# One linear-attention and two-layer kernel: q times kv in three float32r passes, k's maximum row by a transpose, lower parts of blocks 0 and 1 made by TensorE

## The chip, the cores and the metric

The kernel runs on one core of a Trainium2 chip. The metric is the device time of one execution in microseconds. The time before is a median of three runs.

## The reference, cut to what matters

```python
# q, k, v: (8, 8, 576, 64)
q_s = exp(q - max(q, -1)); q_s = q_s / (sum(q_s, -1) + 1e-9)      # over the 64 features
k_s = exp(k - max(k,  2)); k_s = k_s / (sum(k_s,  2) + 1e-9)      # over the 576 rows
kv  = einsum('bhsd,bhse->bhde', k_s, v)
x   = einsum('bhsd,bhde->bhse', q_s, kv)                          # then (4608, 512)
h = x @ w_in;  x1 = where(h > 0, h, exp(min(h, 0)) - 1) @ w_out   # 512 -> 2048 -> 512
h = x1 @ w2_in; out = (P(h) / Q(h)) @ w2_out                      # 512 -> 2048 -> 512
```

All tensors are float32; the weights and the second layer's coefficients are inputs as well.

## The kernel before

The 4608 rows of x are nine blocks of 512 columns (x is kept transposed, features on the partitions). A batch has 576 rows, so block j covers the end of batch j-1 and the beginning of batch j: `pieces(j)` gives the two parts, 16j and 128-16j groups of four columns, that is 64 and 448 columns in block 1, 128 and 384 in block 2, and so on to 448 and 64 in block 7; blocks 0 and 8 are one piece. A block has four pairs of heads (`hp`), of 128 features each.

`plan_pair` makes one pair of one block. For k: the maximum over the rows on VectorE (`k_max`), a transpose on TensorE (`k_maxT`), a maximum over its columns (`k_top`), the result spread into a row for all partitions by a float32 product with the identity (`k_row`, L418), the subtraction (`k_sub`) and the exponential (`k_exp`); `kv_mm` (L433) multiplies with v and a column of ones, `kv_norm` makes the reciprocal, and `kv_div` writes the two 64x64 blocks of the block-diagonal `kvd` on ScalarE (L447) or VectorE (L449). For q: `q_max` to `q_mul` make the softmax, `q_T` (L479) transposes it by four TensorE transposes into a PSUM bank, `q_copy` (L483) copies it out, and `x_mm` (L490) multiplies it with `kvd` in float32. The trace shows a float32 product as two rows and a transpose or a float32r product as one.

Everything after that is float32r: a number is kept as an upper part, which is the float32r rounding (`copy_hi`, L202, on ScalarE), and a lower part, the rest (`sub_lo`, L205, on VectorE or GpSimd), and a product is three passes, upper by upper, upper by lower, lower by upper. `plan_in` (L564 to L566) makes h of 128 hidden features (a step f) in a bank, 12 passes of 512 columns; `plan_elu` makes relu, exp, elu (L673) and the two parts of g; `plan_out` (L605) adds 12 passes into four accumulators. 16 steps make a block. Blocks 0 and 1 take turns, eight steps each, while the weights are loaded and split: `plan_w1` turns two steps' weights at a time into the two parts by VectorE operations on their bits (L232, L241, L246, L251, L255 and L205). The other blocks follow one after the other, and then the second layer, nine blocks again.

The order on every engine is made at build time by `Plan`: each operation has engines with costs, operations it follows, a rank, and buffers that it takes and frees, and the planner issues whichever can start first by its own clock. On the chip each engine then runs its own queue in that order, and waits for others by semaphores. `bank` stands for four PSUM banks, `xs` for eight buffers of an x tile with its two parts, `qe` for the only buffer of the exponential of q.

Of the kernel before, what the change touches and what calls it, by code (L numbers as in the profile page):

```python
# [18 lines left out]
P = 128  # L19
# [84 lines left out]
def linear_attention_elu_rational(  # L104
# [58 lines left out]
    kvd = [at.tile([P, P], F32, name=f"kvd{i}") for i in range(6)]  # L163
# [3 lines left out]
    for name, cap in (("m", 2), ("e", 4), ("bank", 4), ("acc", 4), ("xs", 8), ("gs", 2), ("x", 1), ("st", 1), ("kt", 1),  # L167
                      ("vb", 1), ("qt", 1), ("ke", 1), ("qe", 1), ("km", 2), ("top", 2), ("qT", 1), ("kvd", 6), ("hc", 3),
                      ("s", 3), ("p", 3), ("g2", 2), *((f"w{f}_{i}", 1) for f in range(KF // 2) for i in range(2))):
        plan.kind(name, cap)  # L170
# [178 lines left out]

    def plan_pair(j, hp, r, gate=None):  # L350
# [54 lines left out]
        def k_max(e):  # L405
            km = b["km"] = at.tile([P, 2, D], F32, tag="km", name="km", bufs=2)
            nc.vector.tensor_reduce(out=km, in_=b["kt"].rearrange("p h j d -> p h d j"), op=ALU.max, axis=AX.X)
# [9 lines left out]
        def k_row(e):  # L417
            nc.tensor.matmul(b["mt"][:, P:2 * P], b["top"].to_broadcast([P, P]), ident, start=True, stop=True)  # L418
# [24 lines left out]
        def kv_div(e):  # L443
            for o in (0, 64):
                dst, src, rs = kvd[n % 6][o:o + 64, o:o + 64], b["pk"][o:o + 64, 0:D], b["rs"][o:o + 64]
                if e == "ACT":
                    nc.scalar.activation(out=dst, in_=src, func=AF.Copy, scale=rs)  # L447
                else:
                    nc.vector.tensor_scalar(out=dst, in0=src, scalar1=rs, scalar2=None, op0=ALU.mult)  # L449
# [26 lines left out]
        def q_T(e):  # L476
            pt = b["pt"] = bank()
            for i in range(4):
                nc.tensor.transpose(pt[:, i * P:(i + 1) * P], b["qe"][:, i].rearrange("p h d -> p (h d)"), ident)  # L479

        def q_copy(e):
            b["qT"] = f32_tile("qT", 1, at)
            nc.scalar.activation(out=b["qT"], in_=b["pt"], func=AF.Copy)  # L483

        def x_mm(e):
            px = b["px"] = bank()
            pv = px.rearrange("c (i p) -> c i p", i=4)
            t = b["qT"].rearrange("c (i p) -> c i p", i=4)
            for bb, p0, p1 in pieces(j):
                nc.tensor.matmul(pv[:, :, p0:p1], kvd[(bb * NP + hp) % 6], t[:, :, p0:p1], start=True, stop=True)  # L490

        def x_hi(e):
            x = x_tile[0, j, hp] = main.tile([P, 2, TB], F32R, tag="xs", name="xs", bufs=8)
            copy_hi(x[:, 0], b["px"])
# [14 lines left out]
        t1 = chain("q_T", (PE(0.47), q_T, [o], r + 1.5), take=["bank", "qT"], free=[("qe", qx)], extra=0.2)  # L509
        qc = chain("q_copy", (ACT(), q_copy, [t1], r + 1.7), free=[("bank", t1)], extra=ahead)  # L510

        if j < B:
            pad = chain("pad_k", (DVE(0.2) if first else POOL(0.3), pad_k, (), r - 4 if first else r - 3), take=[kkind])
            l = chain("load_k", ((("SP", 1.1),), load_k, [pad], r - 3), extra=DMA)
            lv = chain("load_v", ((("ACT" if first else "SP", 1.9),), load_v, (), r - 0.6 if first else r - 2), take=[vkind], extra=DMA)
            km = chain("k_max", (DVE(0.8), k_max, [l, gate], r - 0.5), take=["km"])
            mt = chain("k_maxT", (PE(0.2), k_maxT, [km], r - 0.45), take=["bank"], extra=0.2, free=[("km", km)])
            top = chain("k_top", (DVE(0.3), k_top, [mt], r - 0.4), take=["top"], extra=ahead)
            o = chain("k_row", (PE(0.3), k_row, [top], r - 0.35), extra=0.2, free=[("top", top)])
            o = chain("k_sub", (DVE(0.85), k_sub, [o], r + 0.1), free=[("bank", mt)])  # L520
            kx = o = chain("k_exp", (ACT(0.75), k_exp, [o], r + 0.2), take=["ke"], free=[(kkind, pad)], extra=ahead)
            kvm = chain("kv_mm", (PE(1.15), kv_mm, [o, lv], r + 0.5), take=["bank", "kvd"], extra=0.2,
                        free=[("ke", kx), (vkind, lv)])
            o = chain("kv_norm", (DVE(0.4), kv_norm, [kvm], r + 0.7))
            kv_ready[n] = chain("kv_div", ((("ACT", 0.6), ("DVE", 0.4)), kv_div, [o], r + 0.7), free=[("bank", kvm)],
                                extra=ahead)
            kvd_of[n] = kvm
        free = [("qT", t1)]
# [3 lines left out]
        xm = chain("x_mm", (PE(0.9), x_mm, [qc] + need, r + 2), take=["bank", "xs"], extra=0.2, free=free)  # L532
        o = chain("x_hi", (ACT(), x_hi, [xm], r + 2.1))
        x_ready[0, j, hp] = chain("x_lo", (DVE(), x_lo, [o], r + 2.2), free=[("bank", xm)])
        x_owner[0, j, hp] = "xs", xm
# [309 lines left out]
    with tc.manual_schedule():  # L845
# [3 lines left out]
        make_identity(nc, ident)  # L849
        for t in kvd:  # L850
            nc.vector.memset(t, 0.0)
# [57 lines left out]
```

## Time and profile before

| | us |
|---|---|
| median of 3 runs (1730.26 to 1730.96) | 1730.64 |
| the profiled execution | 1730.37 |
| its span in the trace | 1728.6 |
| TensorE busy | 1683.9 |
| VectorE busy | 1075.0 |
| ScalarE busy | 1013.1 |
| GpSimd busy | 822.9 |

The profiled execution lasts 1.8 us longer than its span. TensorE rows overlap (a row of 512 columns reads 390 ns long, and the next begins some 227 ns after it), so what a product costs is read from the starts of the rows around it and not from its length.

### The profile page before, as it was taken

What the parts mean: (1) busy time and instruction counts of PE and PEld (TensorE: products, weight loads), DVE (VectorE), ACT (ScalarE), POOL (GpSimd) and SP (SyncE); (2) the same over time, 40 slices, a digit from 0 to 9 for tenths busy, and PEclk for the clock granted to TensorE, in tenths of its full rate; (3) what the DMA queues carried; (4) which work ended last, traced back from release to release, by engine and by line L of the source; (5) the groups of instructions that cost most, each with busy time, mean ns of one, the idle gap of its engine ahead of it and who ended that gap; (6) DMA issues with size and microseconds to landing.
All of it is one profiled execution on the core that took longest, in us unless ns stands there. A gap on an engine that the chain in (4) does not pass through costs nothing.

```text
span 1728.6 us, 21977 instructions
## 1 busy us (share of the span) xinstructions
PE 1683.9 (97%) x7920; PEld 1372.6 (79%) x7920; DVE 1075.0 (62%) x1500; ACT 1013.1 (59%) x1696; POOL 822.9 (48%) x619
## 2 busy tenths in 40 slices
PE   4799999999999999999999999999999999999999
PEld 3577888888888888888888788888888888888887
DVE  7999656454454544432123867776768676868686
ACT  3565545454444544434456767776868686868675
POOL 2324433433333334323365756564747475757553
PEclk8899999999999999999999999999999999999999
DMA  9710343232322333210233001010101010101000
GB/s 281 253 53 26 124 138 101 76 106 71 110 81 68 103 87 113 69 43 7 74 103 109 26 2 48 1 43 1 49 1 49 1 50 0 50 1 38 0 25 25
DMA packets 110925, 112.58 MB, mean 65 GB/s; under 512 B 48864, under 2 KB 82656, under 8 KB 110816
## 3 DMA queue, kind: packets, MB, share of 16 engines
q1 hardware_dynamic: 106016, 110.00, 20.3%
q10 hardware_dynamic: 4800, 1.18, 0.3%
q8 instruction: 62, 1.02, 0.2%
q14 instruction: 47, 0.39, 0.1%
HBM read 81.79 MB, written 29.36 MB: 64 GB/s over the span
## 4 chain that ended last, share of the span: by engine, by line
PE 88%; DVE 6%; DMA 2%; issue 1%; ACT 1%; POOL 1%; SPq 0%; DVEq 0%; POOLq 0%; ACTq 0%
PE acc L605 43%; PE ps L564 14%; PE ps L566 14%; PE ps L565 14%; PE ps L490 2%; PE ps L433 1%; DMA bits<-in_moe_w_in_dram 1%; PE ps L479 1%; DVE bits L251 1%; DVE x L241 1%; DMA kt<-in_k_dram 0%; DVE x L232 0%; DVE x L255 0%; DVE bits L246 0%; POOL gs L205 0%
## 5 line engine op out<-in xcount | busy, mean ns | idle before, releaser
L564 PE MATMUL ps<-xs,w_in 128*128 128x512 f32 x1152 | 458.3, 398 | 2.8 <-DVE p L727 2.7
L605 PE MATMUL acc<-gs,w_out 128*128 128x512 f32 x1728 | 439.8, 400 | 12.6 <-ACT gs L202 7.7
L566 PE MATMUL ps<-xs,w_in 128*128 128x512 f32 x1152 | 450.8, 391 | 0.0
L565 PE MATMUL ps<-xs,w_in 128*128 128x512 f32 x1152 | 449.7, 390 | 0.0
L605 PEld LDWEIGHTS acc<-gs,w_out 128*128 128x128 f32 x1728 | 321.8, 190 | 85.4 <-ACT gs L202 9.2
L205 POOL TENSOR_TENSOR gs<-m,gs 128x512 fp32r<-128x512 f32 x127 | 173.3, 1364 | 353.8 <-ACT gs L202 304.1
L673 DVE SCALAR_TENSOR_TENSOR m<-m,ps 128x512 f32<-128x512 f32 x144 | 98.5, 684 | 273.5 <-ACT m L670 265.8
L564 PEld LDWEIGHTS ps<-xs,w_in 128*128 128x128 f32 x1152 | 217.3, 189 | 50.8 <-DVE p L727 4.1
L566 PEld LDWEIGHTS ps<-xs,w_in 128*128 128x128 f32 x1152 | 216.9, 188 | 46.5
L565 PEld LDWEIGHTS ps<-xs,w_in 128*128 128x128 f32 x1152 | 217.4, 189 | 44.9 <-issue 0.7
L709 POOL TENSOR_TENSOR s<-s,m 128x512 f32<-128x512 f32 x144 | 218.9, 1520 | 32.2 <-ACT m L698 32.2
L605 PE MATMUL acc<-w_out,g 128*128 128x512 f32 x864 | 211.6, 389 | 0.0
L605 PE MATMUL acc<-w_out,gs 128*128 128x512 f32 x864 | 210.6, 389 | 0.0
L667 ACT ACTIVATE m<-ps 128x512 f32<-128x512 f32 x144 | 85.8, 596 | 207.4 <-PE ps L566 173.4
L605 PEld LDWEIGHTS acc<-w_out,gs 128*128 128x128 f32 x864 | 162.5, 188 | 33.7
L605 PEld LDWEIGHTS acc<-w_out,g 128*128 128x128 f32 x864 | 162.2, 188 | 33.8 <-DVE g L205 0.3
L205 POOL TENSOR_TENSOR g<-p,g 128x512 fp32r<-128x512 f32 x71 | 105.2, 1481 | 173.5 <-ACT g L202 116.4
L718 DVE SCALAR_TENSOR_TENSOR s<-s,m 128x512 f32<-128x512 f32 x144 | 148.1, 1028 | 48.7 <-ACT m L715 34.5
L706 ACT ACTIVATE p<-ps,a_sb 128x512 f32<-128x512 f32 x144 | 112.2, 779 | 109.6 <-PE ps L566 50.6
L202 ACT ACTIVATE gs<-m 128x512 fp32r<-128x512 f32 x144 | 90.6, 629 | 143.5 <-PE acc L605 125.7
L724 DVE TENSOR_TENSOR p<-p,ps 128x512 f32<-128x512 f32 x144 | 98.2, 682 | 85.6 <-ACT s L702 76.5
L727 DVE SCALAR_TENSOR_TENSOR p<-p,a_sb,ps 128x512 f32<-128x512 f32 x144 | 107.3, 745 | 62.6 <-ACT m L698 62.3
(93 smaller groups left out, 2038.1 us busy)
## 6 DMA issues: line engine op xcount, KB each, us to landing
x<-e SPq DMA_DIRECT2D x36, 256.0 KB, 2.1
e<-x SPq DMA_DIRECT2D x36, 256.0 KB, 2.8
out_dram<-e SPq DMA_DIRECT2D x36, 256.0 KB, 2.6
kt<-in_k_dram SPq DMA_DIRECT2D x32, 256.0 KB, 2.8
bits<-in_moe_w_in_dram SPq DMA_DIRECT2D x16, 512.0 KB, 7.8
bits<-in_moe_w_out_dram SPq DMA_DIRECT2D x16, 512.0 KB, 9.7
st<-in_moe_w_in_dram SPq DMA_DIRECT2D x16, 512.0 KB, 4.2
w<-x SPq DMA_DIRECT2D x32, 256.0 KB, 2.1
```

The costliest lines, as they stand in the source:

```text
L202: nc.scalar.activation(out=hi, in_=src, func=AF.Copy)
L205: engine[e].tensor_tensor(out=lo, in0=src, in1=hi.bitcast(F32), op=ALU.subtract)
L564: nc.tensor.matmul(b["h"], w[:, 0, kk, :], x[:, 0], start=(kk == 0), stop=False)
L565: nc.tensor.matmul(b["h"], w[:, 0, kk, :], x[:, 1], start=False, stop=False)
L566: nc.tensor.matmul(b["h"], w[:, 1, kk, :], x[:, 0], start=False, stop=(kk == KD - 1))
L605: nc.tensor.matmul(o, lhsT, rhs, start=(f == f0 and n == 0), stop=(f == f1 and n == 2))
L673: nc.vector.scalar_tensor_tensor(out=b["m"], in0=b["m"], scalar=-1.0, in1=b["h"], op0=ALU.add, op1=ALU.max)
L706: nc.scalar.activation(out=b["p"], in_=b["h"], func=AF.Identity, scale=a_sb[:, 3:4], bias=a_sb[:, 2:3])
L709: engine[e].tensor_tensor(out=b["s"], in0=b["s"], in1=b["a"], op=ALU.add)
L718: nc.vector.scalar_tensor_tensor(out=b["s"], in0=b["s"], scalar=1.0 + 1e-6, in1=b["a"], op0=ALU.add, op1=ALU.mult)
L724: nc.vector.tensor_tensor(out=b["p"], in0=b["p"], in1=b["h"], op=ALU.mult)
L727: nc.vector.scalar_tensor_tensor(out=b["p"], in0=b["p"], scalar=a_sb[:, 1:2], in1=b["h"], op0=ALU.add, op1=ALU.mult)
```

## The change

`k_row` becomes a transpose of the same column. `x_mm` reads a q with two parts and a `kvd` with two parts and makes three float32r passes per piece; the float32 buffer `qT` is gone, and the two parts of q lie in the pair's `xs` buffer, which is now taken at `q_T` and not at `x_mm`. `kv_div` is an upper part on ScalarE (two instructions) and a lower part on VectorE (two instructions) for every pair. In blocks 2 to 8 the lower part of q is a subtraction on VectorE (`q_lo`). In blocks 0 and 1 (`PE_LO`) TensorE makes the lower parts of q and of x in a second bank: it makes the same sum again (four float32 products with the identity, or the three passes again), adds the upper part times minus the identity (`less`), and ScalarE copies what is left (`rest`). The costs given to the planner change with it.

```diff
+    minus = at.tile([P, P], F32R, name="minus")
+    kvd = [at.tile([P, 2, P], F32R, name=f"kvd{i}") for i in range(6)]
...
-            nc.tensor.matmul(b["mt"][:, P:2 * P], b["top"].to_broadcast([P, P]), ident, start=True, stop=True)
+            nc.tensor.transpose(b["mt"][:, P:2 * P], b["top"].to_broadcast([P, P]), ident)
...
+                nc.scalar.activation(out=hi, in_=src, func=AF.Copy, scale=rs)
+                nc.vector.scalar_tensor_tensor(out=lo, in0=src, scalar=rs, in1=hi.bitcast(F32),
+                                               op0=ALU.mult, op1=ALU.subtract)
...
+            if j in PE_LO:
+                pt = b["pt2"] = bank()
+                for i in range(4):
+                    nc.tensor.matmul(pt[:, i * P:(i + 1) * P], b["qe"][:, i].rearrange("p h d -> p (h d)"), ident,
+                                     start=i == 0, stop=False)
...
+        def less(ps):
+            def fn(e):
+                nc.tensor.matmul(b[ps], minus, x_tile[0, j, hp][:, 0], start=False, stop=True)
+            return fn
+
+        def rest(ps):
+            def fn(e):
+                nc.scalar.activation(out=x_tile[0, j, hp][:, 1], in_=b[ps], func=AF.Copy)
+            return fn
...
+            for ps in ("px", "px2") if j in PE_LO else ("px",):
+                b[ps] = bank()
+                pv = b[ps].rearrange("c (i p) -> c i p", i=4)
+                for bb, p0, p1 in pieces(j):
+                    kv = kvd[(bb * NP + hp) % 6]
+                    for m, (kk, qq) in enumerate(((0, 0), (0, 1), (1, 0))):
+                        nc.tensor.matmul(pv[:, :, p0:p1], kv[:, kk], t[:, qq, :, p0:p1],
+                                         start=m == 0 and (p0 == 0 or ps == "px"), stop=m == 2 and ps == "px")
...
+            o = chain("q_less", (PE(0.23), less("pt2"), [o], r + 1.8), free=[("bank", t1)], extra=0.2)
+            qc = chain("q_rest", (ACT(), rest("pt2"), [o], r + 1.9), free=[("bank", t1)])
+        else:
+            qc = chain("q_lo", (DVE(), q_lo, [o], r + 1.8), free=[("bank", t1)], extra=ahead)
...
-        xm = chain("x_mm", (PE(0.9), x_mm, [qc] + need, r + 2), take=["bank", "xs"], extra=0.2, free=free)
+        xm = chain("x_mm", (PE(1.4 if j in PE_LO else 0.7), x_mm, [qc] + need, r + 2), take=["bank"] * (2 if j in PE_LO else 1), extra=0.2, free=free)
```

TensorE's queue, from the products of block 0's second pair to the first step, before (L479 is the transposes of q, L490 x_mm, L433 kv_mm, whose last instance here is that of block 1's first pair, L411 and L418 the two of k, L564 the first step):

```order
L479 MATMUL ps<-ident,qe 128x128 x4
L411 MATMUL ps<-ident,km 128x128
L490 MATMUL ps<-qT,kvd_144 128x512
L479 MATMUL ps<-ident,qe 128x128 x4
L490 MATMUL ps<-qT,kvd_145 128x512
L418 MATMUL ps<-ident,top 128x128
L479 MATMUL ps<-ident,qe 128x128 x4
L433 MATMUL ps<-vb,ke 64x65 x10
L490 MATMUL ps<-qT,kvd_146 128x512
L564 MATMUL ps<-xs,w_in 128x512
```

The same queue of the changed kernel, from block 0's third pair to the first step (L484 is the transposes, L488 the float32 products of the second bank, L501 `less`, L517 x_mm, L437 kv_mm, again that of block 1's first pair, L602 the first step):

```order
L484 MATMUL ps<-ident,qe 128x128 x4
L488 MATMUL ps<-ident,qe 128x128 x4
L437 MATMUL ps<-vb,ke 64x65 x10
L501 MATMUL ps<-xs,minus 128x512
L517 MATMUL ps<-xs,kvd_146 128x512 x6
L501 MATMUL ps<-xs,minus 128x512
L484 MATMUL ps<-ident,qe 128x128 x4
L488 MATMUL ps<-ident,qe 128x128 x4
L602 MATMUL ps<-xs,w_in 128x512
```

Behind kv_mm of block 1's first pair stood one product, x_mm of the fourth pair; now `less`, six passes and `less` of the third pair and the transposes of the fourth stand there, and x_mm of the fourth pair has gone behind the beginning of the first step.

VectorE's queue at `kv_div` of the first pair, before (L439 and L440 are `kv_norm`, L468 and L469 `q_rec`, L415 `k_top` of the third pair):

```order
L439 TENSOR_SCALAR rs<-ps 128x1
L440 RECIPROCAL rs<-rs 128x1
L468 TENSOR_SCALAR sm<-sm 128x8
L469 RECIPROCAL sm<-sm 128x8
L415 TENSOR_REDUCE top<-ps 128x1
```

And in the changed kernel (L443, L444, L473, L474 and L419 are the same five; L453 is the lower part of `kvd`):

```order
L443 TENSOR_SCALAR rs<-ps 128x1
L444 RECIPROCAL rs<-rs 128x1
L473 TENSOR_SCALAR sm<-sm 128x8
L474 RECIPROCAL sm<-sm 128x8
L453 SCALAR_TENSOR_TENSOR kvd_144<-ps,rs,kvd_144 64x64 x2
L419 TENSOR_REDUCE top<-ps 128x1
```

Two instructions that read ScalarE's upper part now stand ahead of `k_top`; the same holds at all 32 pairs.

VectorE's queue around the thirteenth elu (L673, step 4 of block 1), before (L241, L246, L251 and L255 are the splitting of weights):

```order
L241 SCALAR_TENSOR_TENSOR x<-bits,x 128x1024
L232 TENSOR_SCALAR x<-bits 128x1024
L246 TENSOR_SCALAR bits<-bits 128x1024
L251 SCALAR_TENSOR_TENSOR bits<-bits 128x1024
L673 SCALAR_TENSOR_TENSOR m<-m,ps 128x512
L465 TENSOR_REDUCE sm<-qe 128x4x2
L255 TENSOR_TENSOR x<-x,bits 128x1024
L673 SCALAR_TENSOR_TENSOR m<-m,ps 128x512
```

And in the changed kernel (L711 is elu; L242, L247, L252 and L256 the same splitting):

```order
L242 SCALAR_TENSOR_TENSOR x<-bits,x 128x1024
L247 TENSOR_SCALAR bits<-bits 128x1024
L242 SCALAR_TENSOR_TENSOR x<-bits,x 128x1024
L252 SCALAR_TENSOR_TENSOR bits<-bits 128x1024
L247 TENSOR_SCALAR bits<-bits 128x1024
L256 TENSOR_TENSOR x<-x,bits 128x1024
L252 SCALAR_TENSOR_TENSOR bits<-bits 128x1024
L411 TENSOR_REDUCE km<-kt 128x128
L458 TENSOR_REDUCE mx<-qt 128x8
L711 SCALAR_TENSOR_TENSOR m<-m,ps 128x512
```

More of the splitting of weights stands ahead of this elu. Counted from the beginning of the queue to it, the changed kernel has 16 L453 more, the two `kv_div` of VectorE (L449) and eight lower parts of x (L205) less, one subtraction of q more (GpSimd had it), and one more each of the kinds L241, L246, L251 and L255.

## Rows read from the trace of the kernel before

**Rows 1.** The page's first line.

```profile
span 1728.6 us, 21977 instructions
```

**Rows 2.** Busy time by stretch: start:end us, length, each engine, granted TensorE clock.

```profile
16.00:153.00 137.00, 112.89 (x571) 85.02 (x568) 131.18 (x170) 76.36 (x118) 43.42 (x32) 0.91 0.50 162
72.00:82.00 10.00, 5.86 (x14) 4.18 (x14) 9.42 (x12) 4.51 (x7) 5.57 (x3) 0.50 0.81 272
153.00:850.00 697.00, 696.67 (x3511) 565.51 (x3511) 326.52 (x555) 318.43 (x553) 251.00 (x217) 1.00 0.27 82
```

**Rows 3.** Timeline of all engines at 149.0 to 152.8 us: start, length, engine, line.

```profile
149.12 0.68 DVE L673 SCALAR_TENSOR_TENSOR m<-m,ps 128x512 f32<-128x512 f32 x1
...
150.60 2.06 POOL L205 TENSOR_TENSOR gs<-m,gs 128x512 fp32r<-128x512 f32 x1 [3.21 <-ACT gs L202]
...
152.72 0.50 PE L605 MATMUL acc<-gs,w_out 128*128 128x512 f32 x1 [1.64 <-POOL gs L205]
```

**Rows 4.** TensorE's timeline around one k_maxT and one k_row of the long stretch.

```profile
307.49 0.27 PE L411 MATMUL ps<-ident,km 128*128 128x128 f32 x1
...
307.84 0.39 PE L565 MATMUL ps<-xs,w_in 128*128 128x512 f32 x1
308.07 0.40 PE L566 MATMUL ps<-xs,w_in 128*128 128x512 f32 x1
...
313.08 0.38 PE L418 MATMUL ps<-ident,top 128*128 128x128 f32 x2
...
313.53 0.39 PE L565 MATMUL ps<-xs,w_in 128*128 128x512 f32 x1
```

**Rows 5.** TensorE's timeline around x_mm of blocks 3 and 7.

```profile
325.70 1.02 PE L490 MATMUL ps<-qT,kvd 128*128 128x192 f32 x4
...
326.79 0.40 PE L565 MATMUL ps<-xs,w_in 128*128 128x512 f32 x1
...
718.98 1.08 PE L490 MATMUL ps<-qT,kvd 128*128 128x448 f32 x4
...
720.18 0.39 PE L565 MATMUL ps<-xs,w_in 128*128 128x512 f32 x1
```

**Rows 6.** TensorE's timeline around one q_T, four transposes of 128 columns.

```profile
387.06 0.60 PE L479 MATMUL ps<-ident,qe 128*128 128x128 f32 x4
...
387.73 0.40 PE L565 MATMUL ps<-xs,w_in 128*128 128x512 f32 x1
```

**Rows 7.** VectorE's groups between 16 and 150 us: count, busy us, mean ns.

```profile
L251 DVE SCALAR_TENSOR_TENSOR bits<-bits 128x1024 f32<-128x1024 uint32 x13 | 17.8, 1367 | 0.1
L241 DVE SCALAR_TENSOR_TENSOR x<-bits,x 128x1024 int32<-128x1024 int32 x13 | 17.5, 1345 | 0.2
...
L255 DVE TENSOR_TENSOR x<-x,bits 128x1024 f32<-128x1024 f32 x12 | 14.8, 1236 | 0.0
...
L246 DVE TENSOR_SCALAR bits<-bits 128x1024 int32<-128x1024 int32 x13 | 10.0, 769 | 0.0
...
L205 DVE TENSOR_TENSOR xs<-ps,xs 128x512 fp32r<-128x512 f32 x8 | 5.5, 682 | 0.2
```

**Rows 8.** VectorE's and ScalarE's kv_div, groups of the whole span.

```profile
L447 ACT ACTIVATE kvd<-ps,rs 64x64 f32<-64x64 f32 x52 | 15.8, 305 | 7.5 <-DVE rs L440 5.3 <-PE ps L418 1.6
...
L449 DVE TENSOR_SCALAR kvd<-ps,rs 64x64 f32<-64x64 f32 x12 | 3.4, 283 | 0.2
```

**Rows 9.** TensorE's timeline from the last kv_mm ahead of the first step.

```profile
42.23 1.35 PE L433 MATMUL ps<-vb,ke 128*64 128x65 f32 x20 [4.45 <-ACT ke L427]
...
44.60 1.41 PE L564 MATMUL ps<-xs,w_in 128*128 128x512 f32 x1
45.81 0.63 PE L565 MATMUL ps<-xs,w_in 128*128 128x512 f32 x1
46.24 0.63 PE L566 MATMUL ps<-xs,w_in 128*128 128x512 f32 x1
```

**Rows 10.** TensorE's timeline, the output passes after its longest wait.

```profile
76.94 5.06 PE L605 MATMUL acc<-gs,w_out 128*128 128x512 f32 x11 [1.30 <-POOL gs L205]
```

More of the change, by code (lines that the diff above doesn't have):

```diff
@@ L348, in linear_attention_elu_rational @@
     kvd_of = {}
+    PE_LO = (0, 1)
     def plan_pair(j, hp, r, gate=None):
@@ L444, in kv_div @@
             for o in (0, 64):
[L445 to L449, printed above, removed]
+                t = kvd[n % 6]
+                hi, lo = t[o:o + 64, 0, o:o + 64], t[o:o + 64, 1, o:o + 64]
+                src, rs = b["pk"][o:o + 64, 0:D], b["rs"][o:o + 64]
+                nc.scalar.activation(out=hi, in_=src, func=AF.Copy, scale=rs)
+                nc.vector.scalar_tensor_tensor(out=lo, in0=src, scalar=rs, in1=hi.bitcast(F32),
+                                               op0=ALU.mult, op1=ALU.subtract)
         def q_max(e):
@@ L479, in q_T, with q_lo @@
                 nc.tensor.transpose(pt[:, i * P:(i + 1) * P], b["qe"][:, i].rearrange("p h d -> p (h d)"), ident)
-        def q_copy(e):
-            b["qT"] = f32_tile("qT", 1, at)
-            nc.scalar.activation(out=b["qT"], in_=b["pt"], func=AF.Copy)
-        def x_mm(e):
[L486 to L490, printed above, removed]
+            if j in PE_LO:
[3 more added lines that the diff above has]
+                                     start=i == 0, stop=False)
+        def q_copy(e):
+            x = x_tile[0, j, hp] = main.tile([P, 2, TB], F32R, tag="xs", name="xs", bufs=8)
+            copy_hi(x[:, 0], b["pt"])
+        def q_lo(e):
+            x = x_tile[0, j, hp]
+            sub_lo(e, x[:, 1], b["pt"], x[:, 0])
+        def less(ps):
[6 more added lines that the diff above has]
+            return fn
+        def x_mm(e):
+            t = x_tile[0, j, hp].rearrange("c s (i p) -> c s i p", i=4)
+            for ps in ("px", "px2") if j in PE_LO else ("px",):
[6 more added lines that the diff above has]
+                                         start=m == 0 and (p0 == 0 or ps == "px"), stop=m == 2 and ps == "px")
         def x_hi(e):
-            x = x_tile[0, j, hp] = main.tile([P, 2, TB], F32R, tag="xs", name="xs", bufs=8)
+            x = x_tile[0, j, hp]
             copy_hi(x[:, 0], b["px"])
@@ L508, in plan_pair @@
         o = chain("q_mul", (either, q_mul, [o], r + 1.2), extra=ahead)
-        t1 = chain("q_T", (PE(0.47), q_T, [o], r + 1.5), take=["bank", "qT"], free=[("qe", qx)], extra=0.2)
-        qc = chain("q_copy", (ACT(), q_copy, [t1], r + 1.7), free=[("bank", t1)], extra=ahead)
+        t1 = chain("q_T", (PE(1.4 if j in PE_LO else 0.47), q_T, [o], r + 1.5), take=["bank"] * (2 if j in PE_LO else 1) + ["xs"],
+                   free=[("qe", qx)], extra=0.2)
+        o = chain("q_copy", (ACT(), q_copy, [t1], r + 1.7))
+        if j in PE_LO:
+            o = chain("q_less", (PE(0.23), less("pt2"), [o], r + 1.8), free=[("bank", t1)], extra=0.2)
+            qc = chain("q_rest", (ACT(), rest("pt2"), [o], r + 1.9), free=[("bank", t1)])
+        else:
+            qc = chain("q_lo", (DVE(), q_lo, [o], r + 1.8), free=[("bank", t1)], extra=ahead)
         if j < B:
@@ L518, in plan_pair @@
             top = chain("k_top", (DVE(0.3), k_top, [mt], r - 0.4), take=["top"], extra=ahead)
-            o = chain("k_row", (PE(0.3), k_row, [top], r - 0.35), extra=0.2, free=[("top", top)])
+            o = chain("k_row", (PE(0.15), k_row, [top], r - 0.35), extra=0.2, free=[("top", top)])
             o = chain("k_sub", (DVE(0.85), k_sub, [o], r + 0.1), free=[("bank", mt)])
             kx = o = chain("k_exp", (ACT(0.75), k_exp, [o], r + 0.2), take=["ke"], free=[(kkind, pad)], extra=ahead)
-            kvm = chain("kv_mm", (PE(1.15), kv_mm, [o, lv], r + 0.5), take=["bank", "kvd"], extra=0.2,
+            kvm = chain("kv_mm", (PE(0.7), kv_mm, [o, lv], r + 0.5), take=["bank", "kvd"], extra=0.2,
                         free=[("ke", kx), (vkind, lv)])
             o = chain("kv_norm", (DVE(0.4), kv_norm, [kvm], r + 0.7))
-            kv_ready[n] = chain("kv_div", ((("ACT", 0.6), ("DVE", 0.4)), kv_div, [o], r + 0.7), free=[("bank", kvm)],
+            kv_ready[n] = chain("kv_div", (DVE(0.9), kv_div, [o], r + 0.7), free=[("bank", kvm)],
                                 extra=ahead)
             kvd_of[n] = kvm
-        free = [("qT", t1)]
+        free = []
         if j > 0:
```

16 lines of the change are left out of this document (10 added, 6 removed).

## Prediction

> **What bounds the kernel now.** I read the busy times by stretch first, then the timelines at the places where TensorE waits. Between 153 and 850 us TensorE is busy 696.67 of 697 us [rows 2]: what it is spared there comes off the end. Between 16 and 153 us it is idle 137 - 112.89 = 24.1 us while VectorE is busy 131.18 of 137, or 96% [rows 2]. There VectorE sets the pace: it splits the weights, makes the maxima and sums of the softmaxes and the elus, in one queue. The last place where that costs TensorE anything is at 151 to 152.7 us: the thirteenth elu begins on VectorE at 149.12, the lower part of its g ends on GpSimd at 150.60 + 2.06 = 152.66, and TensorE, idle for 1.64 us, goes on at 152.72 [rows 3]. Up to there the reader should count VectorE's queue, and behind it TensorE's products. The sum is made against the profiled execution: a span of 1728.6 us [rows 1], 1730.4 with the 1.8 us around it, which is 0.3 below the median of the runs.
>
> **TensorE's products behind 153 us.** A plain float32r pass takes 308.07 - 307.84 = 0.23 us from start to start [rows 4]. From the start of k_row to that of the second pass behind it are 313.53 - 313.08 = 0.45 us, and from k_maxT, a transpose of the same size, 307.84 - 307.49 = 0.35 [rows 4]. So a row by transpose saves 0.10 us, and 24 of them lie there (blocks 2 to 7): **2.4 us**. A column spread over 128 columns is the stationary operand in both, so I see no reason for another price; if it had none of this gain, the sum would be 2.4 worse.
>
> x_mm in float32 costs 326.79 - 325.70 - 0.23 = 0.86 us in block 3 and 720.18 - 718.98 - 0.23 = 0.97 in block 7, whose second piece has 64 columns [rows 5]. I take 0.86 for blocks 2 to 6 and 8. The three passes I build from two rows. A pass of 512 columns takes 0.23 us, which is 512 / 2.4 = 213 ns of streaming and some 14 ns. And no product with a weight load of its own goes below the transposes of q: (387.73 - 387.06 - 0.23) / 4 = 0.11 us each [rows 6]. With the larger of 0.11 and columns / 2.4 + 14 ns, three passes of both pieces are 3 x (0.11 + 0.17) = 0.85 us in blocks 2 and 6, 3 x (0.11 + 0.15) = 0.77 in 3 and 5, 6 x 0.12 = 0.73 in 4, 3 x (0.11 + 0.20) = 0.93 in 7, and 3 x 0.23 = 0.68 in 8. The savings per pair are 0.01, 0.09, 0.13, 0.09, 0.01, 0.04 and 0.18, times four pairs: **2.2 us**. No float32r pass of fewer than 512 columns is in the trace, so this is bounded from both sides: with streaming alone, 3 x 0.213 = 0.64 us a pair, it would be about 28 x 0.22 + 0.4 = 6.6 us of saving; with passes under 512 columns at float32's four cycles a column, three times 0.86 us, 24 x 1.7 = 41 us of loss. I stay near the row of 512, because float32's price per column does not depend on the width [rows 5].
>
> The lower part of q is one more subtraction on VectorE and the lower part of kvd two more instructions per pair. Behind 153 us VectorE is busy 326.52 of 697 us [rows 2], so that idle half hides them. Their wait for ScalarE delays only what stands behind them on VectorE. The xs buffer taken earlier holds q_T of block 2 back until block 0's last step frees it; behind it stand steps of block 1, so I put it at nothing, with 1 us as the upper bound.
>
> **The start, counted on VectorE's queue.** Up to the thirteenth elu it holds, beside what it held: 16 lower parts of kvd (0.283 us each, the row nearest to them, two to a pair [rows 8]), 4.5 us; one subtraction of q (0.68, as a lower part of x of the same size [rows 7]), 0.7; and one each of four splitting instructions, 1.345 + 0.769 + 1.367 + 1.236 = 4.7 us [rows 7], which the planner has moved ahead of the elu. It no longer holds eight lower parts of x, 8 x 0.682 = 5.5 [rows 7], and two halves of kvd, 0.6 [rows 8]. Together 4.5 + 0.7 + 4.7 - 5.5 - 0.6 = +3.8 us. New waits come on top: the lower part of kvd stands behind two ScalarE instructions of 0.305 us [rows 8]. At three of the eight pairs only the small instructions of q_rec stand between, some 0.3 us short; at the others a longer one does. That is 0.9 us, bounded by 0 and 8 x 0.61 = 4.9. For the price of a lower part the bounds are half of 0.283 and the 0.68 of a lower part of x, so -2.3 to +6.4 us. So the start becomes **4.7 us longer**. What is late next: that elu's g, then TensorE, which has no idle time behind it to give back.
>
> **TensorE in the start.** Its second bank costs, per pair, four float32 products of a k_row's kind, 4 x 0.22 = 0.88 us, two `less` of 0.23, and three passes more, 0.68 or 0.93: 2.0 in block 0 and 2.3 in block 1, 17 us in all; at the lower of its two levels, 1.2 GHz, block 0's are twice that, since a pass of 512 columns takes 46.24 - 45.81 = 0.43 us there [rows 9]. I put them at nothing because 24.1 us of idle time are there to take them. That cover is nearly used up: 4 x 4 + 4 x 2.3 = 25 us if all of block 0 runs at that level. The first step will be late: behind kv_mm at 42.23 there now stand `less`, six passes, `less` and the eight transposes and products of the fourth pair, 0.4 + 2.6 + 0.4 + 0.9 + 1.8 = 6.1 us at that level, so it begins at about 42.23 + 1.35 + 6.1 = 49.7 us in place of 44.60 [rows 9]. The elus are late by as much on VectorE's queue, so I add nothing for it.
>
> **Sum.** 1730.4 - 2.4 - 2.2 + 4.7 = 1730.5; with the 0.3 to the median **1730.8 us**: no change that can be measured. I call 0.2% (3.5 us) the least that a measurement of this kernel tells from none.
>
> **Rivals.** *Narrow passes.* If the narrower piece of each unequal split runs at float32's four cycles a column, 128 columns take 0.21 us and 192 take 0.32 in place of 0.11, and 64 stay at 0.11. Then blocks 2 and 6 lose 8 x 3 x 0.10 = 2.4 us and blocks 3 and 5 lose 8 x 3 x 0.21 = 5.0: 1738.2 us, slower. Against it: float32 at 64 and 448 columns shows no such jump [rows 5]. For it: no row shows the opposite. It decides as soon as a pass of 192 columns costs over 0.2 us. The Trainium skill (PSUM — Partial Sum Buffer, Specifications) says that an output that isn't contiguous slows matmuls significantly, and the pieces are written in four runs; the float32 pieces of this trace, written likewise, do not show it. By that rule the total would be this rival's or worse.
>
> *TensorE becomes the bound of the start.* Its 25 us of new work and 24.1 of idle time are near to each other, and its queue is in order: a `less` that waits for ScalarE holds the steps behind it. If four tenths of that work are not hidden, the start is 10 us longer in place of 4.7: 1736 us, slower. For it: kv_mm already waited 4.45 us for ScalarE [rows 9], and two more pairs stand behind that wait. Against it: a TensorE that is busier keeps its higher level longer.
>
> *The start is not longer.* Of the 3.8 us on VectorE, 4.7 are splitting of weights that has to be done at some time and is only earlier, so later elus meet a shorter queue; if another place than the thirteenth elu binds, the change's own rows are 4.5 + 0.7 - 5.5 - 0.6 = -0.9 us, and with the 0.9 of waits nothing is lost: 1726 us, faster. TensorE's waits also cost it its clock: between 72 and 82 us the granted share is 0.50 [rows 2], and eleven output passes take 5.06 us, 0.46 each in place of 0.23 [rows 10], 2.5 us that more work on TensorE there would win back: 1723.6. The Trainium skill (TensorE: Matmul & The Clock Gate, Part 1) has the full clock released by activity and withdrawn when it stops, and the trace agrees in this stretch. By it alone the sum would be 2.5 us lower.
>
> **How the numbers follow.** The forecast has 0.45 and a range of its own of 1727.5 to 1734; narrow passes 0.13, TensorE as the bound 0.14, a start that is not longer 0.28. The range from 1724.5 to 1738.5 takes in the prices of the three and leaves out some 0.1 below, where the clock is won back too, and 0.07 above, where the narrow passes or the waits cost more. Faster by over 0.2%: 0.28; within: 0.45; slower: 0.13 + 0.14 = 0.27.
>
> **What would show it.** Right: a k_row of one row, 0.35 us from its start to that of the second pass behind it; x_mm's six rows 0.77 us in block 3; no idle time on TensorE between 160 and 850 us; the thirteenth elu at about 154 us. Wrong: passes of 192 columns starting over 0.2 us apart; waits of TensorE for ScalarE's copies of the second bank ahead of 150 us; the thirteenth elu at 149 us or earlier; waits of several us where q_T of block 2 comes late.

## The result and the profile after

The changed kernel takes 1739.8 us (median of 4 runs, 1737.6 to 1741.0) against 1730.45 us, a ratio of 1.0057 with an interval of 1.0045 to 1.0070. It is slower by 0.57%, outside the forecast's range and outside the wider one, which ended at 1738.5. The profiled execution took 1737.6 us, 1.8 more than its span:

```profile
span 1735.8 us, 22366 instructions
```

The busy times by stretch, to be held beside [rows 2]:

```profile
16.00:153.00 137.00, 117.42 (x648) 93.91 (x649) 125.03 (x172) 81.74 (x129) 36.34 (x28) 0.91 0.52 161
72.00:82.00 10.00, 9.79 (x55) 7.68 (x56) 9.49 (x16) 5.85 (x10) 3.52 (x3) 0.83 1.10 309
153.00:850.00 697.00, 693.66 (x3547) 566.37 (x3546) 366.11 (x631) 323.20 (x566) 249.06 (x217) 1.00 0.27 82
```

Between 16 and 153 us VectorE is busy 6.2 us less than before, though it got more to do: it waits. Behind 153 us TensorE, which waited for 0.3 us before, now waits for 3.3. The granted clock of the start is 0.91 as before; what was won between 72 and 82 us was lost elsewhere.

The gains behind the start are there. TensorE's timeline around one k_row and one x_mm of block 3, which answers to [rows 4, 5]:

```profile
311.45 0.94 PE L517 MATMUL ps<-xs,kvd 128*128 128x192 f32 x6
312.23 0.85 PE L643 MATMUL acc<-gs,w_out 128*128 128x512 f32 x3
```

```profile
326.01 0.27 PE L422 MATMUL ps<-ident,top 128*128 128x128 f32 x1
326.03 0.47 PE L602 MATMUL ps<-xs,w_in 128*128 128x512 f32 x1
326.35 0.39 PE L603 MATMUL ps<-xs,w_in 128*128 128x512 f32 x1
```

Six passes take 0.78 us (0.77 forecast), and from the row to the second pass behind it are 0.34 us (0.35). Read in the same way, x_mm of the 28 pairs behind 153 us costs 2.2 us less than before in all, and a row 0.114 us less. The start is what got longer. The timeline around the thirteenth elu, to be held beside [rows 3]:

```profile
159.94 0.67 DVE L711 SCALAR_TENSOR_TENSOR m<-m,ps 128x512 f32<-128x512 f32 x1
...
161.10 2.24 POOL L206 TENSOR_TENSOR gs<-m,gs 128x512 fp32r<-128x512 f32 x1
...
163.40 0.50 PE L643 MATMUL acc<-gs,w_out 128*128 128x512 f32 x1 [2.16 <-POOL gs L206]
```

The elu begins 10.8 us later and TensorE goes on 10.7 us later; forecast were 4.7. The busy times from 0 to this elu say what kind of time it is; the columns are those of [rows 2], first the kernel before, then the changed one:

```profile
0.00:149.12 149.12, 113.84 (x572) 85.67 (x573) 137.40 (x193) 76.42 (x117) 44.35 (x40) 0.92 0.56 173
```

```profile
0.00:159.94 159.94, 126.23 (x683) 100.39 (x684) 140.22 (x204) 86.22 (x135) 41.49 (x37) 0.93 0.53 160
```

VectorE's work grew by 140.22 - 137.40 = 2.8 us and its idle time from 11.7 to 19.7, by 8.0 us. VectorE's groups between 16 and 160 us name the two waits (after the last bar: idle time ahead, and what ended it):

```profile
L470 DVE TENSOR_REDUCE sm<-qe 128x8 f32<-128x512 f32 x8 | 5.5, 682 | 7.6 <-ACT qe L466 7.6
L453 DVE SCALAR_TENSOR_TENSOR kvd<-ps,rs,kvd 64x64 fp32r<-64x64 f32 x16 | 4.5, 283 | 6.0 <-ACT kvd L452 5.9
```

Together these are 13.6 us, of which the kernel before had 0.8, at the same sums over q's exponentials (its L465). Other waits became shorter by some 5 us, which leaves the 8.0; of the two longest that the kernel before had, at `kv_norm` behind kv_mm and at `k_max` behind a load of k, only 1.0 us is left, at kv_mm. The kernel before, up to its thirteenth elu (line, releaser, us in total, times, longest):

```profile
DVE rs L439 <- PE ps L433: 2.4, 1, 2.4
DVE km L407 <- DMA kt<-in_k_dram: 2.3, 2, 1.4
```

The second of the two waits is `kv_div`. Its timeline at the first pair shows four instructions in a row on two engines, each of which waits for the one ahead, ScalarE's second half for VectorE's first too:

```profile
20.73 0.29 ACT L452 ACTIVATE kvd<-ps,rs 64x64 fp32r<-64x64 f32 x1
...
21.06 0.28 DVE L453 SCALAR_TENSOR_TENSOR kvd<-ps,rs,kvd 64x64 fp32r<-64x64 f32 x1 [0.35 <-ACT kvd L452]
21.37 0.31 ACT L452 ACTIVATE kvd<-ps,rs 64x64 fp32r<-64x64 f32 x1 [0.34 <-DVE kvd L453]
21.71 0.29 DVE L453 SCALAR_TENSOR_TENSOR kvd<-ps,rs,kvd 64x64 fp32r<-64x64 f32 x1 [0.38 <-ACT kvd L452]
```

The first of the two waits is at the beginning. ScalarE's timeline of the kernel before, and then of the changed one (ACTq are its DMA issues):

```profile
0.75 1.31 ACTq L386 DMA_DIRECT2D vb<-in_v_dram  x2
...
9.73 1.28 ACT L461 ACT_TABLE_LOAD   x1 [9.73 <-DMA vt<-in_v_dram]
11.03 0.63 ACT L461 ACTIVATE qe<-e 128x512 f32<-128x512 f32 x1
```

```profile
0.74 1.28 ACT L888 ACT_TABLE_LOAD   x1 [0.74 <-PEq L931]
2.03 0.31 ACT L888 ACTIVATE minus<-ident 128x128 fp32r<-128x128 f32 x1
7.31 2.97 ACTq L390 DMA_DIRECT2D vb<-in_v_dram  x2
...
15.81 0.63 ACT L466 ACTIVATE qe<-e 128x512 f32<-128x512 f32 x1 [13.46 <-DMA vb<-in_v_dram]
```

The tile of minus ones is written first and is done at 2.3 us, yet the first load of v is issued at 7.31 in place of 0.75, and the first exponential of q, behind three pairs' loads, comes at 15.81 in place of 11.03. VectorE waits 6.5 us for it, and the first kv_mm starts at 18.64 in place of 15.54.

### The profile page after: what moved, and what is told of

Its sections match the earlier page's. It is cut to its first block, busy times and chain, and to the rows that moved or that the text cites. A ratio compares the mean times of both kernels' runs of the same rounds, so it can differ in the third digit from the quotient of the medians.

```text
span 1735.8 us, 22366 instructions
## 1 busy us (share of the span) xinstructions
PE 1691.5 (97%) x8068; PEld 1387.0 (80%) x8068; DVE 1107.8 (64%) x1576; ACT 1026.0 (59%) x1725; POOL 815.0 (47%) x615
## 4 chain that ended last, share of the span: by engine, by line
PE 87%; DVE 6%; ACT 2%; issue 1%; DMA 1%; POOL 1%; SPq 0%; ACTq 0%; DVEq 0%; POOLq 0%
PE acc L643 43%; PE ps L602 14%; PE ps L604 13%; PE ps L603 13%; PE ps L517 2%; PE ps L437 1%; DVE x L242 1%; PE ps L484 1%; DVE bits L252 1%; DVE x L256 1%; ACT x L238 1%; DVE x L233 0%; POOL gs L206 0%; DVE m L711 0%; DVE km L411 0%
## 5 line engine op out<-in xcount | busy, mean ns | idle before, releaser
L602 PE MATMUL ps<-xs,w_in 128*128 128x512 f32 x1152 | 455.3, 395 | 4.1 <-DVE p L765 2.7
L643 PE MATMUL acc<-gs,w_out 128*128 128x512 f32 x1728 | 431.8, 395 | 4.3 <-POOL gs L206 3.6
L602 PEld LDWEIGHTS ps<-xs,w_in 128*128 128x128 f32 x1152 | 216.5, 188 | 53.1 <-DVE p L765 4.1
L711 DVE SCALAR_TENSOR_TENSOR m<-m,ps 128x512 f32<-128x512 f32 x144 | 98.5, 684 | 209.5 <-ACT m L708 204.8
```

The lines of the kernel that those rows point to most:

```text
L602: nc.tensor.matmul(b["h"], w[:, 0, kk, :], x[:, 0], start=(kk == 0), stop=False)
L643: nc.tensor.matmul(o, lhsT, rhs, start=(f == f0 and n == 0), stop=(f == f1 and n == 2))
L711: nc.vector.scalar_tensor_tensor(out=b["m"], in0=b["m"], scalar=-1.0, in1=b["h"], op0=ALU.add, op1=ALU.max)
```

## The experiments

Each run has the kernel before beside it on the same chip (medians of 1729.9 to 1730.7 us); ratios are to that, with their intervals. Differences between two runs are those of their medians, and single executions of one kernel lie up to 6 us apart, so a difference of 1 us says little. Three claims were set against each other first: A, TensorE's added products lengthen the start; B, VectorE's queue sets its pace; C, the late first load of v is the loss.

**No second bank** (edit of the changed kernel: `PE_LO = ()`).

> The changed kernel with the lower parts of q and x of blocks 0 and 1 subtracted on VectorE as in the other blocks; the unused tile of minus ones is still written at the head of ScalarE's queue. Theory A (TensorE's idle time in the start is waiting inside a chain and no room for more work, so its new products lengthen the start): TensorE loses some 17 us of work, VectorE gains 16 lower parts of 0.68 us = 11 us, and the end comes 5 to 12 us earlier than with the change, 1728 to 1735 us. Theory B (that of the prediction: VectorE's queue sets the pace of the start): the end comes by about those 11 us later, less some 3 us of waits for ScalarE that go with the second bank, 1746 to 1750 us. Theory C (the 3 us by which the first k-times-v product starts later is what is lost): no change beyond 1 us.

1744.9 us, 1.0084 (1.0069 to 1.0099): 5 us slower than with the second bank. A's forecast failed, and B has the sign, with a little less than its size. That the products cost nothing is not shown by it: the edit takes 17 us from TensorE and gives VectorE 11 us at once.

**The tile of minus ones by GpSimd.**

```diff
-        nc.scalar.activation(out=minus, in_=ident, func=AF.Copy, scale=-1.0)
+        nc.gpsimd.tensor_scalar(out=minus, in0=ident, scalar1=-1.0, scalar2=None, op0=ALU.mult)
```

> The changed kernel with the tile of minus ones written by GpSimd in place of ScalarE, so that nothing stands ahead of the loads of v in ScalarE's queue. Theory C: the first load of v is issued at 0.8 us in place of 7.3, the first k-times-v product starts at 15.5 us in place of 18.6, and the end comes 3 us earlier, about 1736.5 us. Theory A (the added products of TensorE are the loss): the early part moves, but the gain is under 1.5 us, because the first step waits for the four pairs' products. Theory B: none, since VectorE's queue has 6.5 us of idle time there.

1735.3 us, 1.0033 (1.0020 to 1.0046): 4.5 us faster than the changed kernel, and the first load of v is issued at 0.73 us:

```profile
0.73 1.31 ACTq L390 DMA_DIRECT2D vb<-in_v_dram  x2
```

C is right, but for half of the loss alone.

**Neither** (both edits, the tile left out).

> The changed kernel without the second bank and without the tile of minus ones: what is left is the three passes, the transposed row and the lower parts on VectorE. Theory A and C together: the gains of the two runs before add, 1725 to 1731 us. Theory B: 1743 to 1747 us. If the gain of this kernel is that of one of the two alone, the other was on no path.

1737.7 us, 1.0049 (1.0032 to 1.0065), 2.4 us slower than the run with the tile by GpSimd, which has the second bank. The whole second bank, some 17 us of products, is cheaper than 16 subtractions of VectorE; its first step, which begins at 55.69 us with the bank and at 45.95 here, does not decide: the thirteenth elu stands at 156.65 and 156.76. But at that elu TensorE waits for 2.1 us with the bank and not at all here, so that elu does not mark the limit of the start in both.

**The row alone** (the kernel before with `k_row` as in the change).

> The kernel before with only the row of k's maximum by a transpose in place of the float32 product. From the trace of the changed kernel a row costs 0.11 us less, 24 of them lie where TensorE is never idle: 2.7 us, so 1727.8 us, by all theories. If it is 1730.5, the saved time is lost again to the order of the work around it.

1726.2 us, 0.9979 (0.9970 to 0.9989). 4.0 us less than before; the expected 2.7 lies in the interval (1.9 to 5.2 us).

For the other half of the loss, claim D: VectorE's waits in `kv_div` are paid. **The two parts of kvd planned apart**, with the tile by GpSimd:

```diff
-            kv_ready[n] = chain("kv_div", (DVE(0.9), kv_div, [o], r + 0.7), free=[("bank", kvm)],
-                                extra=ahead)
+            o = chain("kv_hi", (ACT(0.62), kv_hi, [o], r + 0.7))
+            kv_ready[n] = chain("kv_lo", (DVE(0.6), kv_lo, [o], r + 0.75), free=[("bank", kvm)], extra=ahead)
```

> The kernel with the tile of minus ones written by GpSimd, and besides it the higher parts of kvd (ScalarE) and the lower parts (VectorE) as two steps that are planned apart, so that other instructions of VectorE can stand between. Theory D (VectorE's waits for ScalarE inside this step, 6.0 us up to the thirteenth elu, are a loss of the start): most of them go, and the end comes 3 to 6 us earlier than the 1735.3 us without this edit, about 1731 us. Theory A (TensorE's added products alone): within 1 us of 1735.3.

1726.5 us, 0.9977 (0.9968 to 0.9987): 8.8 us faster than the run with the tile by GpSimd, more than expected. VectorE's waits up to the thirteenth elu (line, releaser, us in total, times, longest), without the edit and with it:

```profile
DVE kvd L453 <- ACT kvd L452: 5.9, 12, 1.2
DVE sm L470 <- ACT qe L466: 2.6, 2, 1.6
```

```profile
DVE rs L443 <- PE ps L437: 2.9, 2, 2.6
DVE km L411 <- DMA kt<-in_k_dram: 1.8, 1, 1.8
DVE sm L472 <- ACT qe L468: 1.0, 2, 0.8
```

The wait at `kvd` is gone, and the elu comes at 152.29 in place of 156.65. TensorE's busy time ahead of 155 us and behind it (columns as in [rows 2]), without the edit and with it:

```profile
0.00:155.00 155.00, 122.76 (x673) 97.21 (x674) 138.96 (x203) 84.49 (x132) 40.34 (x38) 0.93 0.55 165
155.00:300.00 145.00, 139.92 (x719) 113.61 (x719) 101.25 (x166) 71.37 (x125) 49.16 (x42) 1.00 0.34 104
```

```profile
0.00:155.00 155.00, 127.08 (x692) 100.13 (x693) 145.62 (x213) 89.64 (x139) 46.25 (x41) 0.94 0.54 167
155.00:300.00 145.00, 143.67 (x755) 117.24 (x754) 95.27 (x165) 71.89 (x126) 54.00 (x46) 1.00 0.37 112
```

It is idle 4.3 us less ahead of 155 us and 3.8 us less behind, 8.1 of the 9.2 us between the two profiled spans (1733.5 and 1724.3). Behind 155 us its waits of 5.1 us, all for elus, their lower parts or a lower part of xs, shrink to the one of 1.3 at the thirteenth elu. Planned apart, the instructions of all engines also get another order, so this run alone does not say whether the wait or the order was worth the 8.8 us.

**Blocks 0 and 1 in float32** (the core of the edit; `kvf` is a float32 `kvd`, block 1's is split later, from a copy, and from block 2 on the two parts of kvd are planned apart):

```diff
+                if j in F32J:
+                    nc.tensor.matmul(pv[:, :, p0:p1], kvf[(bb * NP + hp) % 6], t[:, :, p0:p1], start=True, stop=True)
```

> Blocks 0 and 1 as in the kernel before (one float32 product, kvd and q in float32, no lower parts of either, nothing at the head of ScalarE's queue); from block 2 on the three passes, and the row of k's maximum by a transpose everywhere. The kvd of block 1 is split later, from a copy, by GpSimd and ScalarE. If the change's loss lies in the start alone and its gains behind it are real, the time is that of the row alone, 1726.2 us, less the 2.0 us of the three passes in blocks 2 to 8: 1724.2 us. If the three passes bring nothing in the whole, 1726.2; if the lower parts of q and kvd cost something behind 160 us too, more.

1732.0 us, 1.0008 (0.9999 to 1.0017). The expectation failed: VectorE waited 7.7 us behind kv_mm at kv_norm, and the thirteenth elu came at 155.47.

**One instruction at the head of ScalarE's queue**, in the kernel before.

```diff
+        nc.scalar.activation(out=minus, in_=ident, func=AF.Copy, scale=-1.0)
```

> The kernel before with one instruction more: a tile of minus ones, used by nothing, written by ScalarE ahead of the loads of v in its queue. Theory C (this alone delays the start): the first load of v is issued at about 7 us in place of 0.8, the first k-times-v product starts about 3 us later, and the end comes 3 to 5 us later, 1733.5 to 1735 us. If the start has room for it: 1730.3 us.

1733.45 us, 1.0017 (1.0008 to 1.0027): 2.75 us slower, a little under the expected 3 to 5. The first load of v is issued at 7.65 us, so one instruction of 0.31 us that nothing reads does it, with the table load of 1.28 us that now stands at the head and not ahead of the first exponential:

```profile
2.03 0.31 ACT L851 ACTIVATE minus<-ident 128x128 fp32r<-128x128 f32 x1
7.65 2.98 ACTq L387 DMA_DIRECT2D vb<-in_v_dram  x2
```

**The second bank in block 1 only** (`PE_LO = (1,)`, tile by GpSimd).

> The kernel with the tile of minus ones written by GpSimd, and the second bank in block 1 only: block 0's lower parts are VectorE's. TensorE has 8 us of work less, VectorE eight subtractions of 0.68 us more, 5.4 us. Theory B (VectorE's queue): 1735.3 + 4 to 5.5, about 1740 us. Theory A (TensorE's products ahead of the first step): 1735.3 - 4 to 8, about 1730 us. If they balance, neither alone sets the start: it is a chain that alternates between them, and either work costs.

1741.3 us, 1.0061 (1.0047 to 1.0075): 6.0 us slower than with both blocks, for 5.4 us more subtractions on VectorE and 8 us less on TensorE. That is what B forecast. But the run with neither, which gives VectorE the subtractions of block 1 as well, is 3.6 us faster than this one, so an instruction of VectorE has no fixed price in the start: the order that the planner makes changes with it.

**The split alone**, the tile still ScalarE's.

> The changed kernel with nothing else but the higher and the lower parts of kvd planned as two steps; the tile of minus ones is still ScalarE's first instruction. Theories C and D together: their losses lie at different places and add, so 1739.8 - 8.8 = 1731 us, and a VectorE that no longer waits at the lower parts of kvd while its wait for the first exponential of q stays at 6 us. If the two overlap, nearer to 1727; if the gain of 8.8 us needed the earlier start, nearer to 1736.

1730.5 us, 1.0000 (0.9991 to 1.0010), as expected: C and D are two losses that add.

**The split without a second bank.**

> No second bank, no tile of minus ones, and kvd's parts planned as two steps: the lower parts of q and x of blocks 0 and 1 are VectorE's. Theory B (VectorE's queue sets the start once the waits are gone): eleven us of subtractions come on top of 1726.5 us, less what TensorE's 17 us gave back when both were changed at once (there the second bank was worth 2.4 us): 1729 to 1734 us. Theory A (TensorE's added products still cost): 1720 to 1725 us.

1729.7 us, 0.9999 (0.9990 to 1.0008): within B's forecast; the second bank is worth 3.2 us here.

**Blocks 0 and 1 in float32, with the planner's old number for kv_mm.**

```diff
-            kvm = chain("kv_mm", (PE(0.7), kv_mm, [o, lv], r + 0.5), take=["bank", "kvd"], extra=0.2,
+            kvm = chain("kv_mm", (PE(1.15), kv_mm, [o, lv], r + 0.5), take=["bank", "kvd"], extra=0.2,
```

> Blocks 0 and 1 in float32 as in the run of that kind, with one number changed: the planner counts 1.15 us for the product of k and v, as in the kernel before, in place of 0.7. Theory E (with the shorter number VectorE's step behind that product is planned too early and waits: 7.7 us up to the thirteenth elu there, 2.4 before): the waits fall to 2 to 3 us and the time is 1724 to 1727 us. If that number is not the cause, 1732 us.

1724.6 us, 0.9968 (0.9956 to 0.9981): the fastest of all, 5.3 us below the kernel before, with a wait of 2.6 us behind kv_mm and the thirteenth elu at 142.38. Most of it is the row's, which alone gave 4.0 us; the 1.6 us between this run and the row alone are not clear of the noise, as the two intervals overlap.

**The same number with the second bank and the split.**

> The second bank, the tile of minus ones from GpSimd and kvd's parts as two steps (1726.5 us), with 1.15 us counted for the product of k and v in the planner in place of 0.7. Theory E: VectorE's waits behind that product (3.0 us up to the thirteenth elu) fall by 1 to 3 us, and so does the time, 1724 to 1725.5 us. Otherwise within 1 us of 1726.5.

1730.7 us, 1.0005 (0.9996 to 1.0014). Missed: 4.2 us slower. The wait behind kv_mm is unchanged (2.9 us), and TensorE waits 2.7 us in place of 1.3 behind 155 us; after a wait of 1.95 us its granted clock is 0.50 from 156.3 to 159.7 us, where it is 1.00 without the number. The number moves the order of the queues, and its sign is not a rule; why this order is the worse one was not followed further. The change itself had lowered this number from 1.15 to 0.7 and had also taken away one of the two buffers of k's maxima (`km`). Neither was put back alone in the changed kernel, so what they cost there is not known.

**The wait or the order?** These two leave the plan of the run with the tile by GpSimd as it is. The first writes kvd in the order upper, upper, lower, lower:

```diff
-                nc.scalar.activation(out=hi, in_=src, func=AF.Copy, scale=rs)
-                nc.vector.scalar_tensor_tensor(out=lo, in0=src, scalar=rs, in1=hi.bitcast(F32),
-                                               op0=ALU.mult, op1=ALU.subtract)
+            for hi, lo, src, rs in parts:
+                nc.scalar.activation(out=hi, in_=src, func=AF.Copy, scale=rs)
+            for hi, lo, src, rs in parts:
+                nc.vector.scalar_tensor_tensor(out=lo, in0=src, scalar=rs, in1=hi.bitcast(F32),
+                                               op0=ALU.mult, op1=ALU.subtract)
```

> The kernel with the tile of minus ones from GpSimd (1735.3 us), every instruction planned as there and in the same order on every other engine; inside the step that writes kvd, ScalarE's two higher parts now stand ahead of VectorE's two lower parts, so that VectorE waits once per pair and not twice. Theory D1 (VectorE's waits in that step are paid in full in the end): the second wait of 0.38 us goes in each of the eight pairs of the start, 3.0 us, and the time is about 1732.3 us. Theory D2 (the 8.8 us came from the new order that the separate planning brings): no change beyond 1 us.

1735.4 us, 1.0026 (1.0015 to 1.0037): no change in the whole. But the edit did less than I had reckoned, since VectorE's one wait is now for two instructions:

```profile
DVE kvd L457 <- ACT kvd L455: 4.8, 6, 1.5
```

The busy times from 0 to the elu (columns as in [rows 2]):

```profile
0.00:155.49 155.49, 125.92 (x681) 100.41 (x682) 139.94 (x204) 85.67 (x134) 41.13 (x38) 0.92 0.55 165
```

The wait is 1.1 us shorter, and the elu comes 156.65 - 155.49 = 1.2 us earlier; but VectorE is idle for only 0.5 us less (15.55 after 16.04), and the other 0.7 are work that took less time (139.94 after 140.61). The second makes the upper parts on VectorE too:

```diff
-                nc.scalar.activation(out=hi, in_=src, func=AF.Copy, scale=rs)
+                nc.vector.tensor_scalar(out=hi, in0=src, scalar1=rs, scalar2=None, op0=ALU.mult)
```

> As the run before it, but the higher parts of kvd are VectorE's too, so that the step holds no wait for another engine. Theory D1: the 6.0 us of waits up to the thirteenth elu go and sixteen instructions of 0.28 us, 4.5 us, come: 1.5 us less than 1735.3, 1733.8 us, and some 1 us less than that for the waits of block 2. Theory D2: 4.5 us more work on VectorE and the old order, 1736 to 1740 us.

1734.7 us, 1.0023 (1.0014 to 1.0033). The busy times from 0 to the elu, with the upper parts on ScalarE and on VectorE:

```profile
0.00:156.65 156.65, 124.41 (x681) 98.55 (x682) 140.61 (x205) 85.98 (x134) 40.34 (x38) 0.93 0.54 164
```

```profile
0.00:155.18 155.18, 123.00 (x681) 97.94 (x682) 144.13 (x220) 80.81 (x118) 40.24 (x38) 0.95 0.54 165
```

VectorE works 3.5 us more and idles 16.04 - 11.05 = 5.0 less, and the elu is 1.5 us earlier. The last follows from the other two, since work and idle time make up the time to the elu. What the run shows is that, of the 5.9 us of waits at `kvd`, some 5 us did not come back as other waits up to there. In the whole neither of the two differs from the run with the tile by GpSimd by more than such runs differ anyway (0.1 us slower and 0.6 faster). Taken at face value, a step without waits paid for 3.5 us of work and 0.6 more, some 4 us; that the rest of the 8.8 us came with the new order is inferred, and no run shows it by itself.

**Sixteen more instructions of VectorE in the kernel before.**

```diff
+                nc.vector.tensor_scalar(out=junk[o:o + 64, o:o + 64], in0=src, scalar1=rs, scalar2=None, op0=ALU.mult)
```

> The kernel before with two VectorE instructions more per pair: the two halves of the product of k and v, scaled, into a tile that nobody reads, behind the halves of kvd. They read what the lower parts of kvd read and cost about the same, with no wait for ScalarE's result; the plan is that of before. Theory B as the prediction has it (VectorE's queue in the start is paid one to one): 16 x 0.28 = 4.5 us more, 1735 us. If the queue has slack: 1730 to 1732 us.

1739.8 us, 1.0057 (1.0042 to 1.0072): 9.7 us slower, twice the 4.5 expected. The edit adds two instructions to each of the 32 pairs, 64 in all; 16 of them lie ahead of the thirteenth elu.

```profile
0.00:156.94 156.94, 115.09 (x572) 86.45 (x573) 141.66 (x209) 76.65 (x117) 44.87 (x40) 0.89 0.54 165
```

VectorE's work up to the elu grew by 141.66 - 137.40 = 4.3 us; but they wait too:

```profile
DVE junk L451 <- ACT kvd L448: 3.5, 10, 0.4
```

4.3 + 3.5 = 7.8 us, and the elu is 156.94 - 149.12 = 7.8 us later: the other waits, taken together, did not shrink to make room for them. Behind 155 us, where the other 48 lie, TensorE waits for 5.7 us in place of 0.3; 1.6 of them are the wait at this elu, which lay ahead of 155 us before. The sixteen use nothing that ScalarE writes, but read the bank that it reads, and in this program the two take turns.

## Why the prediction was wrong

**What failed.** The step "New waits come on top": I had it at 0.9 us, bounded by 0 and 8 x 0.61 = 4.9. Up to the thirteenth elu it measured 6.0 us. I counted only ScalarE's two instructions ahead of VectorE's; they alternate, with a hand-over between each two, and ScalarE may come late besides (the longest wait is 1.2 us). Planned apart, they gave 8.8 and 9.3 us back in two kernels, though a part of that may be the new order. A second wait stands in no term of the sum: the tile of minus ones in front of v's loads, 4.0 and 4.5 us in two kernels (1730.5 to 1726.5, 1739.8 to 1735.3). I had counted each engine's instructions, but of the changed order at ScalarE's head, loads included, nothing. Up to the elu the sum had 3.8 us of work and 0.9 of waits; the trace has 2.8 of work, 6.0 of waits at `kvd`, 7.6 - 0.8 = 6.8 more for the exponentials of q, and 4.8 less of other waits: 10.8 in place of 4.7. The two edits together make 8.8 + 4.5 = 13.3 us, more than the 9.0 by which the forecast was missed. Without both the kernel stands at 1726.5, the time of the rival of a start that is not longer, but not for its reason: the thirteenth elu still comes later than before, at 152.29 in place of 149.12, and TensorE still waits there.

**VectorE's queue, +3.8 us of work.** The direction was right, and the work grew by 2.8 us. In two runs more work for VectorE cost its own length or more: 6.0 us for 5.4 with the bank in block 1 only, and 9.7 us with the added instructions. That it is paid one to one everywhere is not shown: 11 us of subtractions, with 17 us of products spared on TensorE, cost 5.1, 2.4 and 3.2 us. A lower part of kvd costs 0.283 us, as taken from [rows 8].

**TensorE's second bank at nothing.** Not shown by itself, since no run adds or takes these products alone. With the 17 us of products, or with 11 us of subtractions in their place, the thirteenth elu stands at 156.65 or 156.76. The first step came still later than I had it, at 58.49 in place of 49.7 [rows 9]; no run shows a loss from that alone. The waits for the second bank's copies that I named as a sign are there (0.75 us at 63.95 us, for a `less` behind the copy of x's upper part). But the cover was not used as I had it: by the page's sums TensorE is idle for 1735.8 - 1691.5 = 44.3 us, and was for 1728.6 - 1683.9 = 44.7. What the products took of the idle time came back as other waits; in the run without the two losses it is 1724.3 - 1687.8 = 36.5. The rival *TensorE becomes the bound* had a start 10 us longer, near the 10.8 that came, but taking products off TensorE and giving VectorE their work made the kernel slower all four times.

**The products behind the start**, 2.4 and 2.2 us: right, with 24 x 0.114 = 2.7 and 2.2 in the trace. The row measures 0.34 us and block 3's x_mm 0.78. One reason that I gave does not hold: float32's price does depend on the width, 0.97 us where a piece has 64 columns against 0.86 [rows 5]. *Narrow passes*, whose 1738.2 us were nearest to the result, is refuted, and its time was luck: six passes over 192 and 320 columns, each written in four runs, cost what their columns say. The Trainium skill (PSUM — Partial Sum Buffer, Specifications) says that an access that isn't contiguous slows matmuls significantly; these 0.78 us against the 0.77 worked out show nothing of it.

**Behind the thirteenth elu** I expected no idle time on TensorE beyond 160 us; it is 3.1 us between 155 and 300, 2.2 of them at that elu and the rest at later ones. q_T of block 2, put at nothing, shows no wait there.

**The clock.** Between 72 and 82 us TensorE is busy 9.79 us in place of 5.86, and the granted clock rose from 0.50 to 0.83. Earlier, from 45.4 to 58.9 us, where TensorE waits 5.0 of 13.5 us, it is 0.50, that is 1.2 GHz:

```profile
45.40:58.90 13.50, 8.49 (x41) 6.39 (x42) 12.58 (x18) 6.72 (x11) 2.30 (x2) 0.50 0.65 207
```

The Trainium skill (TensorE: Matmul & The Clock Gate, Part 1) says that activity releases the full clock; both stretches agree with it. What the rival had won at the one place was lost again at the other: the mean of the start is 0.91 in both kernels.

## What to carry to other kernels

On an engine that sets the pace, count its waits like its instructions: a step that goes to and fro between two engines costs the sum of both and the hand-overs; here it was cheaper planned as two steps with other work between them. Look at what stands ahead of the first loads in each queue, above all at constants that look free. And a change that saves on one engine behind the start and costs on another inside it is worth splitting by place: here the old form in the first two blocks and the new one behind them beat both, though only with one of the two planner numbers tried, and most of the gain came from the transposed row.

## What was not expected of the hardware

The issue of v's first load waited from 2.3 to 7.3 us with no row that it waited for; in that time SyncE issued one load behind another (twelve from 0.75 to 7.86 us, no gap above 0.1), where before its row has gaps of over 1 us and the two queues took turns. Something that the two share in issuing would fit this, but it was not tested.

A wait of TensorE of 2.0 us, near 965 us in the kernel before, stands in the traces of both kernels and of every run. In eight of these seventeen traces 3.4 us at 1.2 GHz follow it, in the other nine none. The kernel before (start, end, columns as in [rows 2]):

```profile
964.50:966.00 1.50, 1.10 (x5) 0.93 (x6) 1.50 (x3) 1.17 (x3) 1.50 (x2) 1.00 0.00 0
966.10:969.40 3.30, 3.30 (x9) 2.53 (x9) 2.54 (x4) 2.70 (x5) 3.30 (x3) 0.50 0.00 0
```

The changed kernel, which waits at 973.75 us, has 1.00 there throughout. Half of such a stretch, 1.7 us, is an estimate of what it costs, and one of the differences between runs that a claim of 1 or 2 us has to clear here.
